# Chunk 0 of a retention block followed by an MLP: part 3 of w_in loaded ahead of the rows of batch 3, and M1 of chunk 0 reordered around it

## The chip, the cores and the metric

The kernel runs on one core of one Trainium2 chip. A core has five engines, each with its own in-order instruction stream: TensorE (matrix products, PE in the profile; PEld is its loading of weights), VectorE (DVE), ScalarE (ACT), GpSimd (POOL) and SyncE (SP, which here only issues DMAs). Engines wait for each other by semaphores. TensorE writes its results to PSUM[...]; VectorE or ScalarE must read ("evict") a bank before it can be used again. The metric is the device time of one execution, in microseconds, lower is better.

## The reference

Two layers, one after the other, in float32:

```python
# q, k, v: (4 batches, 8 heads, 768 steps, 64)
for t in range(768):
    state = gamma[h] * state + outer(k[t], v[t])        # 64 x 64 per batch and head
    y[t] = scale * q[t] @ state
x = y as (4 * 768 tokens, 512)
h = x @ w_in                                            # 512 x 2048
g = 0.5 * h * (1 + tanh(c * (h + 0.044715 h^3)))        # gelu
out = g @ w_out                                         # 2048 x 512
```

gamma is 1 - 2^(-5-head), and scale is 1/8.

## The kernel before, in words

**Tiling.** The 768 steps are cut into 6 chunks of 128. A chunk holds 4 batches of 128 tokens, so 512 tokens. All of a chunk's attention, then M1 (x times w_in, with gelu), then M2 (times w_out) is done before its result is stored; the attention of the next chunks is laid between the products of the chunk at hand. Operands are float16, accumulation is float32.

**Attention of one chunk and batch.** `prep1` casts the rows to float16 with the decay factors (L159, or L143 where a plain copy is enough). `mm_T` transposes q and k on TensorE (L188), 4 head pairs each, into one PSUM bank, and `ev_T` evicts it to `qkT`. `mm_A` multiplies k and q to scores (L208); `ev_A` evicts them with the causal mask (L221). `mm_yi` multiplies the scores with v (L243), `mm_yc` adds what comes from the earlier state (L230; nothing in chunk 0), and `ev_Y` evicts the result to `xT`, the transposed input of M1. `mm_s` multiplies k with v (L267) and `ev_S` folds it into the state. Each `ev_` function takes the engine that does it: VE is VectorE, AC is ScalarE.

**M1.** d_ff = 2048 is 16 blocks of 128 rows (fc). A block of h needs 4 matmuls (kc), one per 128 rows of w_in (L351). Two helpers cut the tokens of chunk 0: `moe1_two` does two blocks for 256 tokens (8 matmuls of 256 columns), `moe1_four` does four blocks for the 128 tokens of one batch (16 matmuls of 128 columns). Both fill one bank of the two with tag "h", and one gelu on ScalarE (L371) empties it into `g`. The token ranges are `t01` (batches 0 and 1), `t2`, `t3` and, before the change, `t23` (batches 2 and 3).

**M2.** The product g times w_out is done with seven products of half-size blocks in place of eight. `g_sums` and `w_sums` make the sums of blocks of g and of w_out that it needs (L401, results `s_g` and `t_w`). For chunk 0 the products are in `units_0`, a list of 15 units; most products are at L632, those at L665 follow after a bank has been kept. Unit 6 ends the first product and keeps it as `s_p` (a ScalarE copy, L643); unit 7, the first at L665, goes on in the same bank. The call of `run(units_0(), ...)` gives for each unit what is done after it: after unit 3 `preps(1, 0)`, the casts of q and k of chunk 1, batch 0, on ScalarE; after unit 5 `att_T(0)`, the transposes of chunk 1, batch 0, with their eviction.

**The order** is written out by hand, line by line, and each engine does its own instructions in that order. Loads of rows come from SP and ACT at first. The weights are cast from float32 to float16 on their way, by DMAs that GpSimd issues: w_in in four parts of 4 blocks each (part 1 in two halves; the code counts from 0, so `load_w_in(2)` is the third part), then w_out in four parts. Rows of batch 3 and of chunk 1 are issued by GpSimd as well, in one stream with the weights. GpSimd also casts k of batch 3 (`prep1(PO, "k", 0, 3)`), and stands at that cast until the row has come; the loads of w_out are behind it. The `spin` calls are products of zeros, whose result nobody reads.

Of the kernel before, what the change touches and what calls it, by code (L numbers as in the profile page):

```python
# [16 lines left out]
def kernel(  # L17
# [11 lines left out]
    C = 128  # L29
# [4 lines left out]
    NF = d_ff // 128  # L34
# [44 lines left out]
    def ld_tile(nm, c, b):  # L79
        if (nm, c, b) not in raw:  # L80
            tag, n = ("v1" if nm == "v" else "qk1", 5 if nm == "v" else 8) if c == 1 else (f"{nm}32", 4)
            raw[nm, c, b] = ld.tile([128, H, Dh], F32, tag=tag, bufs=n, name=f"{nm}32")
        return raw[nm, c, b]
# [30 lines left out]
    def spin(n):  # L114
        ps = bank("h", shape=(128, 512), name="spin_ps")
        for _ in range(n):
            nc.tensor.matmul(
                out=ps, lhsT=zero[:, 0:128], rhs=zero, start=True, stop=True
            )
# [21 lines left out]
    def copy_on(eng, out, in_):  # L141
        if eng is nc.scalar:
            eng.copy(out=out, in_=in_)  # L143
        else:
            eng.tensor_copy(out=out, in_=in_)

    def prep1(eng, nm, c, b):
        if nm == "v":
            t = pre.tile([128, H, Dh], F16, tag="v16", bufs=6, name="v16")
        else:  # L150
            if (c, b) not in qk16:
                qk16[c, b] = pre.tile([128, 2, H, Dh], F16, tag="qk16", bufs=6, name="qk16")
            t = qk16[c, b][:, "qk".index(nm)]
        src = ld_tile(nm, c, b)
        if (nm == "v") == (c < 1):
            copy_on(eng, t, src)
        else:
            col = OQ if nm == "q" else OK
            eng.tensor_tensor(  # L159
                out=t,  # L160
                in0=src,
                in1=cst[:, col:col + H].unsqueeze(2).broadcast_to([128, H, Dh]),
                op=ALU.mult,
            )
        h16[nm, c, b] = t
# [11 lines left out]
    def bank(tag, dt=F32, shape=(128, NHP, 128), name="ps"):  # L177
        return psum.tile(list(shape), dt, tag=tag, bufs=BANKS[tag], name=name)
# [24 lines left out]
    def mm_A(c, b):  # L203
        t = qkT[c, b]
        ps = [bank("att", name=f"a_ps{j}") for j in range(2)]
        for hp in range(NHP):
            for j in range(2):
                nc.tensor.matmul(  # L208
                    out=ps[j][:, hp],
                    lhsT=t[j * 64:(j + 1) * 64, 1, hp],  # L210
                    rhs=t[j * 64:(j + 1) * 64, 0, hp],
                    start=True,
                    stop=True,
                )
        pss["A", c, b] = ps

    def ev_A(c, b):
        ps = pss.pop(("A", c, b))
        for j in range(2):
            s = att.tile([128, NHP, 128], F16, tag=f"a{j}", bufs=2, name=f"a_sb{j}")  # L220
            nc.vector.tensor_tensor(out=s, in0=ps[j], in1=mask[:, j], op=ALU.mult)  # L221
            a_sb[c, b, j] = s

    def mm_yc(c, b, tag):
        y_ps = pss["Y", c, b] = bank(tag, name="y_ps")
        if c == 0:
            return

        for hp in range(NHP):
            nc.tensor.matmul(  # L230
                out=y_ps[:, hp],
                lhsT=st[:, b, hp].rearrange("p j d -> p (j d)"),
                rhs=qkT[c, b][:, 0, hp],
                start=(hp == 0),
                stop=False,
                skip_group_check=True,
            )
# [14 lines left out]
    def ev_Y(c, b, eng=nc.vector):  # L252
        if c not in xT:
            xT[c] = xp.tile([128, NHP, B * C], F16, tag="x", bufs=2, name="xT")
        x, ps = xT[c][:, :, b * C:(b + 1) * C], pss.pop(("Y", c, b))
        if c < 1:
            copy_on(eng, x, ps)
        else:
            nc.vector.tensor_tensor(out=x, in0=ps, in1=dec, op=ALU.mult)  # L259
# [15 lines left out]
    def ev_S(c, bs, engs=(nc.vector, nc.vector)):  # L275
        if c + 1 >= NCk:
            return
        s_ps = pss.pop(("S", c, bs))
        for j in range(2):
            sl = slice(j * 64, (j + 1) * 64)  # L280
            t = st[sl, bs[0]:bs[-1] + 1, :, j]
            if c == 0:
                copy_on(engs[j], t, s_ps[sl])
                continue
            for hp in range(NHP):
                nc.vector.scalar_tensor_tensor(  # L286
                    out=t[:, :, hp],
                    in0=t[:, :, hp],
                    scalar=cst[sl, OG + hp:OG + hp + 1],
                    in1=s_ps[sl, :, hp],  # L290
                    op0=ALU.mult,
                    op1=ALU.add,
                )
# [35 lines left out]
    def load_w_in(i, r0=0, r1=4):  # L329
        n0 = w_in_at[i] + r0  # L330
        nc.gpsimd.dma_start(  # L331
            out=w_in_sb[i][:, :, r0 * 128:r1 * 128],
            in_=moe_w_in.rearrange("(kc p) n -> p kc n", p=128)[
                :, :, n0 * 128:(n0 + r1 - r0) * 128
            ],
        )
# [41 lines left out]
    def moe1_two(c, fp, t0, t1):  # L378

        h_ps = bank("h", shape=(128, 2, B * C // 2), name="h_ps")  # L380
        for r in range(2):
            moe1_mm(c, 2 * fp + r, h_ps[:, r, 0:t1 - t0], t0, t1)
        gelu(g_tile(c, 2 * fp)[:, :, t0:t1], h_ps[:, :, 0:t1 - t0])

    def moe1_four(c, fq, t0, t1):
        h_ps = bank("h", shape=(128, 4, C), name="h_ps")
        for r in range(4):
            moe1_mm(c, 4 * fq + r, h_ps[:, r], t0, t1)
        r0 = fq % 2 * 4
        gelu(g_sb[fq // 2][:, r0:r0 + 4, t0:t1], h_ps)  # L390
# [12 lines left out]
    def w_sums(i):  # L403
        t = {j: t_w[j][:, 2 * i:2 * i + 2] for j in t_w}
        tt(nc.vector, t[1], w_q(i, 0, 1), w_q(i, 0, 0), ALU.subtract)
        tt(nc.vector, t[3], w_q(i, 1, 1), w_q(i, 0, 1), ALU.subtract)
        tt(nc.vector, t[2], w_q(i, 1, 1), t[1], ALU.subtract)
        tt(nc.vector, t[4], w_q(i, 1, 0), t[2], ALU.subtract)

    def g_sums(eng, c, f0, f1, p0=0, p1=2, keys=(1, 2, 3, 4)):  # L410
        i = f0 % 4
        q = {
            (r, b): g_q(c, r, b, f0 // 4)[:, i:i + f1 - f0, p0:p1]
            for r in range(2)
            for b in range(2)
        }
        t = {j: s_g[j][:, f0:f1, p0:p1] for j in s_g}
        ops = (
            (1, q[0, 1], q[1, 1], ALU.add),
            (2, t[1], q[0, 0], ALU.subtract),  # L420
            (3, q[0, 0], q[0, 1], ALU.subtract),
            (4, q[1, 0], t[2], ALU.subtract),
        )
        for j, in0, in1, o in ops:
            if j in keys:
                tt(eng, t[j], in0, in1, o)
# [284 lines left out]
    def loads(eng, c, *what):  # L711
        for nm, b in what:
            load1(eng, nm, c, int(b))
# [7 lines left out]
    VE, AC, PO, SY = nc.vector, nc.scalar, nc.gpsimd, nc.sync  # L721
    half = 2 * C
# [9 lines left out]
    prep1(PO, "k", 0, 1)  # L732
    load_w_in(0, 2, 4)
    load_w_in(1)
    loads(PO, 0, "k3", "q3", "v3")
    load_w_in(2)
    load_w_in(3)
    prep1(PO, "k", 0, 3)
    for i in range(NO):
# [9 lines left out]
    ev_T(0, 1, AC)  # L749
    prep1(AC, "v", 0, 0)  # L750
    spin(4)
    mm_A(0, 1)
    ev_A(0, 1)
    mm_yc(0, 0, "o")
    mm_yi(0, 0)
    prep1(AC, "v", 0, 1)
    ev_Y(0, 0, AC)
    prep1(VE, "q", 0, 2)
    prep1(VE, "k", 0, 2)
    spin(3)  # L760
    mm_yc(0, 1, "o")
    mm_yi(0, 1)
    mm_s(0, (0, 1), "o")
    ev_Y(0, 1, AC)
    spin(2)

    t01, t2, t3, t23 = (0, half), (half, half + C), (half + C, 2 * half), (half, 2 * half)
    moe1_two(0, 0, *t01)
    mm_T(0, 2)
    ev_T(0, 2)  # L770
    prep1(AC, "v", 0, 2)
    moe1_two(0, 1, *t01)
    mm_A(0, 2)
    ev_A(0, 2)
    ev_S(0, (0, 1), (AC, VE))
    moe1_two(0, 2, *t01)
    mm_yc(0, 2, "o")
    mm_yi(0, 2)
    ev_Y(0, 2)
    moe1_two(0, 3, *t01)  # L780
    prep1(VE, "q", 0, 3)
    moe1_four(0, 0, *t2)
    mm_T(0, 3)
    ev_T(0, 3)
    prep1(AC, "v", 0, 3)
    moe1_four(0, 1, *t2)
    mm_A(0, 3)
    ev_A(0, 3)
    g_sums(VE, 0, 0, 4, 0, 1)
    moe1_two(0, 4, *t01)  # L790
    moe1_two(0, 5, *t01)
    mm_yc(0, 3, "o")
    mm_yi(0, 3)
    mm_s(0, (2, 3))
    ev_Y(0, 3)
    ev_S(0, (2, 3))
    moe1_two(0, 6, *t01)
    moe1_two(0, 7, *t01)

    nc.gpsimd.tensor_copy(out=dec[0:1, 0, 0:1], in_=w_out_sb[3][0:1, 0, 0:1])  # L800
    nc.sync.dma_start(out=dec.rearrange("p h t -> p (h t)"), in_=dec_h.ap())
# [4 lines left out]
    g_sums(VE, 0, 4, 8, 0, 1)  # L806
    for fq in range(2):
        moe1_four(0, fq, *t3)
    w_sums(1)
    g_sums(VE, 0, 0, 4, 1, 2)  # L810
    for fp in range(4, NF // 2):
        moe1_two(0, fp, *t23)

    def prep_kT(c, b):
        prep1(AC, "k", c, b)
# [30 lines left out]
    def rows_of(c):  # L846
        for b in range(B):
# [6 lines left out]
            0: [(g_sums, VE, 0, 4, 8, 1, 2), (w_sums, 2)],  # L854
            1: [(w_sums, 3)],
            3: [(preps, 1, 0)],
            5: [(att_T, 0)],
            6: [(preps, 1, 1)],
            7: [(att_1A, 0)],
            8: [(att_T, 1), (preps, 1, 2)],  # L860
# [214 lines left out]
```

## Time and profile before

The time is 202.81 us, the median of 3 runs (202.48 to 202.95). The profiled execution has a span of 200.5 us.

| Engine | Busy, us | Share of the span |
|---|---|---|
| TensorE (PE) | 192.2 | 96% |
| weight load (PEld) | 153.2 | 76% |
| VectorE | 135.0 | 67% |
| ScalarE | 117.1 | 58% |
| GpSimd | 136.5 | 68% |

| Stretch, us | TensorE busy | VectorE | ScalarE | GpSimd |
|---|---|---|---|---|
| 0 to 13 | 10.47 | 6.62 | 5.71 | 9.93 |
| 13 to 26 | 11.08 | 8.64 | 6.25 | 8.35 |
| 26 to 33 | 7.00 | 6.05 | 4.68 | 2.15 |
| 33 to 40 | 6.76 | 6.39 | 2.71 | 5.22 |
| 40 to 60 | 20.00 | 16.78 | 12.09 | 10.62 |

How to read it: the first table is an average over the whole; the second shows where TensorE is not full. A stretch in which an engine is busy for its whole length sets the pace there; in the others it waits for something, and the chain of waits and the timeline tell for what. Busy times of TensorE include the overlap of its pipeline, so a full stretch is not the peak of the unit.

In lines of the profile, `out<-in` are the names of tiles in the code, "x16" is a number of instructions, and the bracket at the end is the idle time just before and what ended it.

### The profile page before, as it was taken

Reading aid. Unit: us, or ns where it says so; the run is one execution under the profiler, and the core shown is the slowest. Engines: PE = TensorE matmul, PEld = TensorE weight load, DVE = VectorE, ACT = ScalarE, POOL = GpSimd, SP = SyncE. Lnnn points to the kernel's source line nnn. Section 1 sums busy time; section 2 is a strip of 40 time slices with the busy share of each in tenths; the row PEclk is TensorE's granted clock in tenths of the full one; section 3 lists DMA queues with packets and bytes.
Section 4 is the critical chain, followed back from the end, with each engine's and each line's share of the span. In section 5 each row is a group of like instructions: output and inputs, shape, how many; then the busy total and the mean of one; then the engine's idle time right before and its main releaser. Section 6 shows DMA issues by size and latency. Waiting matters only on the chain.

```text
span 200.5 us, 5124 instructions
## 1 busy us (share of the span) xinstructions
PE 192.2 (96%) x2070; PEld 153.2 (76%) x2070; DVE 135.0 (67%) x281; ACT 117.1 (58%) x213; POOL 136.5 (68%) x139
## 2 busy tenths in 40 slices
PE   7797899999999999999999999999999999999993
PEld 2365798887887888745577888888888888888882
DVE  3566789869792459995996965995835935227720
ACT  2464554563689419255748698289484495867211
POOL 6782943845199999669969429299979299598100
PEclk9999999999999999999999999999999999999999
DMA  7999999999998899999999589830400220002204
GB/s 159 284 216 272 206 206 253 344 336 207 307 227 163 202 219 224 198 274 261 217 212 239 121 200 216 143 147 32 105 3 0 105 108 0 3 0 106 108 26 183
DMA packets 84743, 34.25 MB, mean 171 GB/s; under 512 B 76976, under 2 KB 81968, under 8 KB 84720
## 3 DMA queue, kind: packets, MB, share of 16 engines
q1 hardware_dynamic: 72736, 18.91, 43.1%
q0 software_dynamic: 7392, 13.37, 25.6%
q10 hardware_dynamic: 4592, 1.65, 3.2%
q8 instruction: 16, 0.26, 0.5%
q14 instruction: 7, 0.06, 0.1%
HBM read 27.63 MB, written 6.29 MB: 169 GB/s over the span
## 4 chain that ended last, share of the span: by engine, by line
PE 84%; DMA 8%; POOL 3%; DVE 2%; ACT 1%; issue 1%; SPq 1%; DVEq 0%
PE o_ps L512 31%; PE h_ps L594 19%; PE h_ps L351 18%; DMA w_in<-in_moe_w_in_dram 5%; PE o_ps L632 3%; PE y_ps L243 3%; PE a_ps L208 3%; PE o_ps L665 3%; DMA k<-in_k_dram 3%; PE y_ps L230 2%; PE s_ps L267 1%; DVE a_sb L221 1%; PE qkT_ps L188 1%; POOL w_in L331 1%; POOL qk L159 1%; DVE xT L259 1%
## 5 line engine op out<-in xcount | busy, mean ns | idle before, releaser
L351 PE MATMUL h_ps<-xT,w_in 128*128 128x256 f16 (+2 forms) x352 | 45.9, 282 | 1.7 <-DMA w_in<-in_moe_w_in_dram 1.5
L371 ACT ACTIVATE g<-h_ps 128x512 f16<-128x512 f32 x52 | 30.9, 599 | 22.5 <-PE h_ps L351 20.8
L221 DVE TENSOR_TENSOR a_sb<-a_ps,mask 128x512 f16<-128x512 f32 x48 | 30.5, 682 | 15.4 <-PE a_ps L208 12.8
L401 POOL TENSOR_TENSOR s_g<-g 128x512 f16<-128x512 f16 x30 | 35.2, 1180 | 7.5 <-ACT g L371 6.5
L351 PEld LDWEIGHTS <-w_in 128*128 128x128 f16 x352 | 30.4, 98 | 12.8 <-DMA w_in<-in_moe_w_in_dram 2.4
L512 PEld LDWEIGHTS <-s_g 128*128 128x128 f16 x320 | 30.6, 98 | 4.2 <-POOL s_g L401 0.3
L371 ACT ACTIVATE g<-h_sb 128x512 f16<-128x512 f32 x36 | 21.9, 632 | 17.4 <-DVE h_sb L401 17.3
L512 PE MATMUL o_ps<-t_w,s_g 128*128 128x256 f16 x240 | 29.4, 273 | 0.0
L401 DVE TENSOR_TENSOR h_sb<-h_ps,h_sb 128x512 f32<-128x512 f32 x36 | 22.8, 682 | 9.6 <-ACT h_sb L143 8.9
L159 POOL TENSOR_TENSOR v<-v,cst 128x512 f16<-128x512 f32 x20 | 20.5, 1046 | 4.3 <-PE y_ps L230 2.5
L512 PEld LDWEIGHTS <-g 128*128 128x128 f16 x208 | 20.2, 98 | 2.5
L401 POOL TENSOR_TENSOR s_g<-s_g,g 128x512 f16<-128x512 f16 x18 | 20.9, 1162 | 1.4
L401 POOL TENSOR_TENSOR s_g<-g,s_g 128x512 f16<-128x512 f16 x18 | 20.6, 1156 | 0.0
L594 PEld LDWEIGHTS <-t_in 128*128 128x128 f16 x192 | 18.0, 98 | 2.9
L143 ACT COPY h_sb<-h_ps 128x512 f32<-128x512 f32 x36 | 19.1, 598 | 1.3 <-PE h_ps L594 1.3
L512 PE MATMUL o_ps<-w_out,g 128*128 128x256 f16 x160 | 19.1, 273 | 0.0
L286 DVE SCALAR_TENSOR_TENSOR st<-st,cst,s_ps 64x128 f16<-64x128 f16 x64 | 18.2, 346 | 0.2
L594 PE MATMUL h_ps<-s_x,t_in 128*128 128x256 f16 x144 | 17.8, 273 | 0.0
L259 DVE TENSOR_TENSOR xT<-y_ps,dec 128x512 f16<-128x512 f32 x20 | 13.3, 682 | 5.4 <-PE y_ps L243 5.4
L594 PEld LDWEIGHTS <-w_in 128*128 128x128 f16 x144 | 14.1, 98 | 1.8
L143 ACT CAST qk<-q 128x512 f16<-128x512 f32 x20 | 12.6, 630 | 3.0 <-DMA q<-in_q_dram 3.0
L401 POOL TENSOR_TENSOR s_g<-g,g_odd 128x512 f16<-128x512 f16 x6 | 6.9, 1153 | 9.0 <-ACT h_sb L143 9.0
(83 smaller groups left out, 274.3 us busy)
## 6 DMA issues: line engine op xcount, KB each, us to landing
out_dram<-o_sb POOLq DMA_DIRECT2D x10, 512.0 KB, 3.1
k<-in_k_dram SPq DMA_DIRECT2D x19, 256.0 KB, 4.7
v<-in_v_dram SPq DMA_DIRECT2D x18, 256.0 KB, 4.2
q<-in_q_dram SPq DMA_DIRECT2D x16, 256.0 KB, 4.7
w_out<-in_moe_w_out_dram POOLq DMA_DIRECT2D x4, 512.0 KB, 10.6
w_in<-in_moe_w_in_dram POOLq DMA_DIRECT2D x3, 512.0 KB, 10.0
k<-in_k_dram POOLq DMA_DIRECT2D x5, 256.0 KB, 8.8
q<-in_q_dram POOLq DMA_DIRECT2D x5, 256.0 KB, 8.6
```

The costliest lines, as they stand in the source:

```text
L143: eng.copy(out=out, in_=in_)
L159: eng.tensor_tensor(out=t, in0=src, in1=cst[:, col:col + H].unsqueeze(2).broadcast_to([128, H, Dh]), op=ALU.mult,)
L208: nc.tensor.matmul(out=ps[j][:, hp], lhsT=t[j * 64:(j + 1) * 64, 1, hp], rhs=t[j * 64:(j + 1) * 64, 0, hp], start=True, stop=True,)
L221: nc.vector.tensor_tensor(out=s, in0=ps[j], in1=mask[:, j], op=ALU.mult)
L243: nc.tensor.matmul(out=y_ps[j * 64:(j + 1) * 64, hp], lhsT=h16["v", c, b][:, 2 * hp + j], rhs=a_sb[c, b, j][:, hp], start=(c == 0), stop=True,
L259: nc.vector.tensor_tensor(out=x, in0=ps, in1=dec, op=ALU.mult)
L286: nc.vector.scalar_tensor_tensor(out=t[:, :, hp], in0=t[:, :, hp], scalar=cst[sl, OG + hp:OG + hp + 1], in1=s_ps[sl, :, hp], op0=ALU.mult, ...
L351: nc.tensor.matmul(out=out, lhsT=w_in_sb[wi][:, kc, wr * 128:(wr + 1) * 128], rhs=xT[c][:, kc, t0:t1], start=(kc == 0), stop=(kc == NHP - ...
L371: nc.scalar.activation(out=out, in_=in_, func=AF.Gelu_apprx_tanh, scale=1.0)
L401: eng.tensor_tensor(out=out, in0=in0, in1=in1, op=op)
L512: nc.tensor.matmul(out=po, lhsT=lhs(c, lk, fp, a), rhs=rhs(rk, fp), start=(new and fp == 0 and (last or a == 0)), stop=(stop and fp == NP ...
L594: nc.tensor.matmul(out=self.ps[G, k][:, p], lhsT=self.lhs(lk, 2 * G + p, kc), rhs=self.rhs(rk, kc), start=(new and p == 0 and kc == 0), st ...
```

## The change

The third part of w_in is issued ahead of the rows of batch 3 instead of behind them. M1 of chunk 0 is put in another order: batches 0 to 2 are multiplied with the first three parts of w_in before the pieces of batch 3, and batch 3 (t3) is done for all 16 blocks at the end, in four units of four blocks; the units for t23 are gone. The casts of q and k of batch 2 on VectorE, and the cast of its v on ScalarE, are put earlier; two spins are dropped. Three kinds of eviction go from VectorE to ScalarE: y of batch 3, both halves of the state of batches 2 and 3, and the transposes of batch 0 of chunk 1. The purpose is to give TensorE work on the weights that have come while it waits for the rest.

```diff
@@ loads
     load_w_in(0, 2, 4)
     load_w_in(1)
+    load_w_in(2)
     loads(PO, 0, "k3", "q3", "v3")
-    load_w_in(2)
     load_w_in(3)
     prep1(PO, "k", 0, 3)
@@ attention of batches 0 and 1, then M1
     spin(4)
+    prep1(VE, "q", 0, 2)
     mm_A(0, 1)
     ev_A(0, 1)
+    prep1(VE, "k", 0, 2)
     mm_yc(0, 0, "o")
     mm_yi(0, 0)
     prep1(AC, "v", 0, 1)
     ev_Y(0, 0, AC)
-    prep1(VE, "q", 0, 2)
-    prep1(VE, "k", 0, 2)
     spin(3)
...
     ev_Y(0, 1, AC)
-    spin(2)
-
-    t01, t2, t3, t23 = (0, half), (half, half + C), (half + C, 2 * half), (half, 2 * half)
-    moe1_two(0, 0, *t01)
+    prep1(AC, "v", 0, 2)
+
+    t01, t2, t3 = (0, half), (half, half + C), (half + C, 2 * half)
     mm_T(0, 2)
     ev_T(0, 2)
-    prep1(AC, "v", 0, 2)
-    moe1_two(0, 1, *t01)
+    moe1_two(0, 0, *t01)
     mm_A(0, 2)
     ev_A(0, 2)
-    ev_S(0, (0, 1), (AC, VE))
-    moe1_two(0, 2, *t01)
+    moe1_two(0, 1, *t01)
     mm_yc(0, 2, "o")
     mm_yi(0, 2)
     ev_Y(0, 2)
+    ev_S(0, (0, 1), (AC, VE))
+    moe1_two(0, 2, *t01)
+    moe1_four(0, 0, *t2)
     moe1_two(0, 3, *t01)
+    g_sums(VE, 0, 0, 4, 0, 1)
+    moe1_four(0, 1, *t2)
     prep1(VE, "q", 0, 3)
-    moe1_four(0, 0, *t2)
+    moe1_two(0, 4, *t01)
+    moe1_two(0, 5, *t01)
     mm_T(0, 3)
     ev_T(0, 3)
     prep1(AC, "v", 0, 3)
-    moe1_four(0, 1, *t2)
+    moe1_four(0, 2, *t2)
     mm_A(0, 3)
     ev_A(0, 3)
-    g_sums(VE, 0, 0, 4, 0, 1)
-    moe1_two(0, 4, *t01)
-    moe1_two(0, 5, *t01)
+    moe1_two(0, 6, *t01)
+    moe1_two(0, 7, *t01)
     mm_yc(0, 3, "o")
     mm_yi(0, 3)
     mm_s(0, (2, 3))
-    ev_Y(0, 3)
-    ev_S(0, (2, 3))
-    moe1_two(0, 6, *t01)
-    moe1_two(0, 7, *t01)
+    ev_Y(0, 3, AC)
+    ev_S(0, (2, 3), (AC, AC))
+    moe1_four(0, 3, *t2)
@@ end of M1
     for fq in range(2):
         moe1_four(0, fq, *t3)
+    g_sums(VE, 0, 0, 4, 1, 2)
     w_sums(1)
-    g_sums(VE, 0, 0, 4, 1, 2)
-    for fp in range(4, NF // 2):
-        moe1_two(0, fp, *t23)
+    for fq in range(2, 4):
+        moe1_four(0, fq, *t3)
@@ M2 of chunk 0, what follows unit 5
-            5: [(att_T, 0)],
+            5: [(att_T, 0, AC)],
```

## The prediction

> **What bounds the kernel now.** I read the page first: TensorE is busy for 192.2 of 200.5 us, and the stage table gives it 20.00 of the 20 us from 40 to 60, 39.85 of 40 from 60 to 100, and all of 100 to 190. Only the opening has holes: 10.47 of 13 us, then 11.08 of 13, and 6.76 of the 7 us from 33 to 40. So whatever moves the opening's end moves the whole. Next the chain that ended last, for the opening; columns are start, length, and what the time went to:
>
> ```profile
> 12.60 10.02 DMA w_in<-in_moe_w_in_dram
> 22.62 0.05 issue
> 22.67 1.94 PE h_ps L351 x16
> ...
> 25.27 7.20 PE h_ps L351 x80
> 32.47 5.24 PE o_ps L632 x48
> 37.71 0.45 PE qkT_ps L188 x8
> 38.15 0.45 PE o_ps L632 x4
> 38.60 0.02 issue
> 38.62 0.59 ACT s_p L643
> 39.22 0.04 issue
> 39.26 1.03 PE o_ps L665 x8
> ```
>
> The third part of w_in lands at 22.62. From 25.27 TensorE is solid to 38.6, waits for one copy (s_p) on ScalarE, and goes on at 39.26. What frees it at 25.27 is in the timeline (start, length, engine, instructions, idle before):
>
> ```profile
> 22.67 1.64 PEld L351 LDWEIGHTS <-w_in 128*128 128x128 f16 x16 [0.56 <-DMA w_in<-in_moe_w_in_dram]
> ...
> 25.26 6.92 PEld L351 LDWEIGHTS <-w_in 128*128 128x128 f16 x80 [0.19 <-DMA w_in<-in_moe_w_in_dram]
> ...
> 26.35 0.60 ACT L371 ACTIVATE g<-h_ps 128x512 f16<-128x512 f32 x1 [1.12 <-PE h_ps L351]
> 27.22 0.60 ACT L371 ACTIVATE g<-h_ps 128x512 f16<-128x512 f32 x1 [0.28 <-PE h_ps L351]
> 28.11 0.60 ACT L371 ACTIVATE g<-h_ps 128x512 f16<-128x512 f32 x1 [0.30 <-PE h_ps L351]
> 29.01 0.60 ACT L371 ACTIVATE g<-h_ps 128x512 f16<-128x512 f32 x1 [0.30 <-PE h_ps L351]
> 29.88 0.60 ACT L371 ACTIVATE g<-h_ps 128x512 f16<-128x512 f32 x1 [0.28 <-PE h_ps L351]
> ```
>
> The fourth part of w_in lands at about 25.25; its DMA was issued at 13.35 and took 11.9. So the gate is the arrival of the last part, not the order of TensorE before it. The gelu starts are a ruler: a unit of 8 matmuls of 256 columns takes 27.22-26.35 = 0.87 us, one of 16 matmuls of 128 columns 29.01-28.11 = 0.90. A gelu begins 1.08 us after its unit (26.35-25.27).
>
> The last view is a comparison of one kind of eviction on two engines:
>
> ```profile
> 6.30 1.01 ACT L143 COPY qkT<-qkT_ps 128x1024 f16<-128x1024 f16 x1 [1.01 <-PE qkT_ps L188]
> ...
> 38.19 0.69 DVE L145 COPY qkT<-qkT_ps 128x1024 f16<-128x1024 f16 x1
> 38.62 0.58 ACT L643 COPY s_p<-o_ps 128x512 f32<-128x512 f32 x1 [1.12 <-PE o_ps L632]
> ```
>
> The transposed q and k of chunk 1 are evicted by VectorE while ScalarE, idle for 1.12 us, waits to take s_p.
>
> [...] The trace agrees with an ordered stream: w_in parts at 16.95, 22.62 and 25.25, batch 3's rows between the first two at 18.8, 19.4 and 20.1.
>
> **The change part by part.**
>
> *The DMA order.* Part 3 of w_in (512 KB) now goes ahead of three row loads (256 KB each). Queue time, from landings: a w_in part 2.5 to 2.6 us (25.25-22.62), the three rows 3.15 (20.1-16.95). So part 3 lands at 16.95+2.6 = 19.5, k of batch 3 at 21.3, q at 22.0, v at 22.7, and part 4 again at 25.25: the same bytes stand before it. The queue stays fed, because part 4 is still issued at about 13.3. Behind it, GpSimd casts k of batch 3 (1.04 us) before it issues w_out; that cast moves from 18.79 to about 21.3, w_out's first issue from 19.78 to 22.4. Part 4 occupies the queue to about 25, so I take no gap; the other bound is in the rivals.
>
> *Before the gate.* TensorE has after 12.4 us: six wide units (6 x 0.87), three narrow ones (3 x 0.90), two sets of transposes (0.45 each, from the chain) and two of scores (0.33), one of y (0.34), in all 9.8 us against 12.9 to the gate. The dropped two spins (0.6 us busy) and the earlier units fall in this slack. The q cast of batch 2 moves ahead of an eviction on VectorE, but q landed at 3.88+5.9 = 9.8 and the cast (0.69) ends at 10.5, when the eviction could start at 10.46: nothing. Batch 3's last pieces: q cast by 22.7, transposes to 23.15, unit of part 3 to 24.05, scores to 24.4. All done 0.85 before the gate. These edits cost and bring nothing: waiting for part 4 hides them.
>
> *After the gate, TensorE.* Before: eight units, 6 wide and 2 narrow: 6 x 0.87 + 2 x 0.90 = 7.02. After: two wide and five narrow units, plus y and the state product of batch 3, which used to lie ahead of the gate (0.34 and 0.37): 1.74+4.5+0.71 = 6.95. So 0.07 less (0.1 with unrounded gelu starts).
>
> *After the gate, ScalarE.* Here three evictions are added: y of batch 3 and both halves of the state product. In ScalarE's order they stand between the second wide unit's gelu and the next one. Starts on ScalarE follow each other 0.49 to 0.52 us apart (gelu 13.93, cast 14.43; gelu 15.55, cast 16.05). The second gelu starts at 27.22, y at 27.72, the state halves at 28.21 and 28.70, and only then the first narrow unit's gelu, at 29.2 to 29.8. That unit is multiplied by 28.6, and the next, in the other of two banks, by 29.5. The third narrow unit needs the first's bank and waits to 29.84: 0.3 us. Its successors lose nothing more. Sum at the end of M1: +0.3-0.1 = +0.2 us. If ScalarE took the full durations one after the other (0.60, 0.58, 0.57, 0.57) the wait would be 0.75; if the states came late behind the gelu, none. I take +0.2, and keep -0.1 and +0.65.
>
> VectorE loses these evictions (3 x 0.69), but its s_g sums for batches 2 and 3 now stand ahead of w_sums(1) and wait for the gelu of the second t3 unit, which ends at 31.5. From there it has g_sums (1.4 us), w_sums(1) (1.5), g_sums (1.4), w_sums(2) and (3) (1.5 each): the operand t_w[2] of the first L665 product is complete at about 38.5, and that product starts at 39.9. The first product with a t_w operand (L632, at 34.3) needs the first operation of w_sums(1), done at 33.4. Nothing, by 0.9 us or more.
>
> *The eviction of chunk 1's first transposes moves to ScalarE.* This one is on the path. Transposes begin at 37.54 in the timeline (the chain's 37.71 deducts overlap); an eviction starts 0.65 later (38.19); on ScalarE the following copy can start 0.91 after it (6.30 apart: in the opening 8.96 to 9.87). So s_p starts at T+1.56 and, at 0.58+0.06, TensorE goes on at T+2.20. Before: 39.26-37.54 = T+1.72. Cost +0.48. Queued behind it on ScalarE are the casts of the next batch (39.11), wanted only at 41.4, and what waits for it is the product at L665, the whole of TensorE.
>
> An earlier T couldn't help much either: the last cast of chunk 1's k starts at 36.89, 0.14 idle after its predecessor, as its row landed at 36.87, and ends at 37.51, when the transposes begin. The rows bound that point to within 0.05 us.
>
> Sum: +0.2+0.5 = +0.7 us; 202.81+0.7 = 203.5. After 39.26 TensorE has no idle time that would take it up.
>
> **The rivals.** (1) *The queue runs dry.* If k of batch 3 lands only with v (22.7), GpSimd issues w_out at 23.8[...]. Chunk 1's rows come that much later, the transposes wait some 0.6: 204.1. For it: GpSimd waits for k now for 4.63 us with w_out behind it. Against it: w_out's first part landed 2.5 after part 4, back to back, with 3 us of lead. (2) *The evictions on ScalarE fit.* No bank wait; M1 ends 0.1 earlier; the handover of s_p costs 0.48: +0.4, 203.2, at the edge of no change. (3) *The gate moves.* Part 4 and the rows behind it arrive earlier, because the rows next to part 3 move better in the new place, and TensorE's fuller slack then counts. To beat both costs the stream must gain over 0.8 us; 1.3 us gained gives 202.3, faster. For it: k of batch 3 took 1.8 us after part 2, q and v 0.65 each, so the change of kind costs something. Against it: there are as many such changes in the new order.
>
> **How the numbers follow.** Forecast +0.7 (203.3 to 203.8): 0.6. Rival 1: 0.13. Rival 2: 0.13. Rival 3: 0.14. The range leaves out most of rival 3 and the far end of rival 1: 202.7 to 204.3; the full ScalarE times (+0.65+0.48 = 203.9) lie in it. Bound of no change is 0.4 us: faster takes rival 3 (0.14), the same takes most of rival 2 (0.12), slower the rest (0.74).
>
> **What would show it.** In the changed kernel: part 4 released at 25.2 to 25.3; three ScalarE copies between two gelus near 28; a TensorE wait for ScalarE inside the narrow units of 0.3 us; the 1.01 us copy of qkT on ScalarE just ahead of s_p; the first L665 product at about 39.95. A last part that lands at 24.5, or that product at 39.3 or sooner, makes me wrong.

## The result and the profile after

The changed kernel takes 205.1 us (median of 4 runs, 204.67 to 205.37) against 202.84: slower by 2.3 us, ratio 1.0113 with a 95% interval of 1.0090 to 1.0135. The profiled executions differ by 3.0 us in span (203.5 and 200.5). In part of the runs of some experiments TensorE's granted clock is lowered (in the profiled ones it falls to half for 3.4 or 6.8 us in the opening), and most of these take 1 to 6 us longer; medians below are of all runs, ratios leave out runs over 1.5% above the kernel's fastest.

First the chain that ended last, of the changed kernel (start, length, what the time went to):

```profile
10.50 10.36 DMA k<-in_k_dram
20.86 0.07 issue
20.93 1.04 POOL qk L159
21.97 2.97 POOL w_out L340 x4
24.95 0.85 POOL q L86
25.80 13.78 DMA k<-in_k_dram
39.58 0.02 issue
39.60 0.63 ACT qk L143
40.23 0.05 issue
40.28 0.41 PE qkT_ps L188 x4
40.69 0.02 issue
40.71 1.01 ACT qkT L143
41.72 0.50 ACT s_p L643
42.22 0.04 issue
42.26 1.03 PE o_ps L665 x8
```

Before, a part of w_in (the third, as the chain has it) and then TensorE itself made this chain. Now it runs from batch 3's k, over GpSimd's cast and the issue of w_out behind it, to the row of chunk 1's k, which lands at 39.58 instead of 36.87. M1 and M2's first units are no longer on it.

The rate at which the DMA engines moved data is the last column of the table by stretches (busy times of the engines, then TensorE's clock, DMA share, GB/s). The kernel before:

```profile
22.00:24.00 2.00, 1.61 (x21) 1.30 (x18) 1.65 (x4) 0.83 (x2) 2.00 (x4) 1.00 1.24 206
24.00:26.00 2.00, 1.92 (x37) 1.51 (x35) 2.00 (x5) 0.95 (x2) 1.99 (x3) 1.00 1.24 206
26.00:28.00 2.00, 2.00 (x29) 1.89 (x28) 1.19 (x3) 1.19 (x2) 0.39 (x1) 1.00 1.26 212
```

The changed kernel:

```profile
22.00:24.00 2.00, 1.18 (x11) 0.81 (x9) 1.95 (x5) 1.45 (x4) 2.00 (x3) 1.00 1.04 170
24.00:26.00 2.00, 1.96 (x34) 1.74 (x35) 0.77 (x2) 0.72 (x2) 2.00 (x4) 1.00 0.98 142
26.00:28.00 2.00, 2.00 (x30) 1.64 (x30) 1.21 (x2) 1.01 (x3) 2.00 (x3) 1.00 1.13 157
28.00:30.00 2.00, 2.00 (x51) 1.96 (x46) 0.96 (x3) 1.96 (x5) 1.19 (x2) 1.00 1.13 183
```

From 22 to 32 the stream carries 376 KB less than before (five stretches of 2 us: 170, 142, 157, 183, 192 against 206, 206, 212, 202, 206), which at 206 GB/s is 1.8 us of the 2.7 by which chunk 1's k is late: about 1.0 from 22 to 26, where the queue runs dry, and 0.85 in the slow stream after it. That is the hole that the prediction said would not be there. Another 0.65 us comes last: k lands 1.41 us after q of the same batch (39.58 and 38.17), before the change 0.76. The hole isn't the reason for this; in e3, below, which has the same loads, it is 0.77, and in e10, which has no hole, 1.59.

TensorE's own path is late too. The timeline of the kernel before:

```profile
16.98 0.77 PEld L351 LDWEIGHTS <-w_in 128*128 128x128 f16 x8 [1.31 <-DMA w_in<-in_moe_w_in_dram]
37.10 0.60 PE L632 MATMUL o_ps<-w_out,s_g 128*128 128x256 f16 x4
37.54 0.61 PE L188 MATMUL qkT_ps<-iden,qk 128*128 128x128 f16 x8
```

The changed kernel:

```profile
17.72 5.18 PEld L351 LDWEIGHTS <-w_in 128*128 128x128 f16 x64 [1.62 <-DMA w_in<-in_moe_w_in_dram]
21.20 1.05 DVE L401 TENSOR_TENSOR s_g<-g 128x512 f16<-128x512 f16 x1 [3.49 <-ACT g L371]
23.30 0.68 DVE L159 TENSOR_TENSOR qk<-q,cst 128x512 f16<-128x512 f32 x1
24.04 0.45 PEld L188 LDWEIGHTS <-qk 128*128 128x128 f16 x8 [1.14 <-DVE qk L159]
25.82 1.64 PEld L351 LDWEIGHTS <-w_in 128*128 128x128 f16 x16
30.59 2.84 PE L351 MATMUL h_ps<-xT,w_in 128*128 128x128 f16 x48 [0.36 <-ACT g L371]
33.26 1.91 PE L632 MATMUL o_ps<-w_out,g 128*128 128x256 f16 x16
38.07 0.60 PE L632 MATMUL o_ps<-w_out,s_g 128*128 128x256 f16 x4
38.87 0.23 PEld L188 LDWEIGHTS <-qk 128*128 128x128 f16 x4 [0.48 <-ACT qk L143]
```

Part 2 of w_in releases TensorE at 17.72 (16.98 before). The cast of batch 3's q stands on VectorE behind four sums, which wait for a gelu until 21.20, though q landed at 21.6; so the transposes start at 24.04, and the first unit of part 4 at 25.82, with no wait for a DMA: the part landed at 24.85 (13.15+11.7). M2 begins at 33.26 instead of 32.30.

The 3.0 us at the first L665 product (42.26 against 39.26) split as follows. TensorE reaches the transposes of chunk 1 at 38.51 (38.07 and a unit of 0.44) instead of 37.54: +0.97. The transposes of k start at 40.28 instead of 0.22 after that, because the row is late: +1.55, of which 0.65 is the gap between q and k. The product follows them by 1.98 instead of 1.50, because of the eviction on ScalarE: +0.48.

### The profile page after: what moved, and what is told of

Same layout as the page of the kernel before. It is cut to its first block, busy times and chain, and to the rows that moved or that the text cites. A ratio compares the mean times of both kernels' runs of the same rounds, so it can differ in the third digit from the quotient of the medians.

```text
span 203.5 us, 5181 instructions
## 1 busy us (share of the span) xinstructions
PE 192.5 (95%) x2100; PEld 153.7 (76%) x2100; DVE 132.6 (65%) x277; ACT 119.6 (59%) x217; POOL 136.3 (67%) x139
## 3 DMA queue, kind: packets, MB, share of 16 engines
q10 hardware_dynamic: 4592, 1.65, 3.1%
## 4 chain that ended last, share of the span: by engine, by line
PE 76%; DMA 14%; POOL 4%; DVE 2%; ACT 1%; issue 1%; SPq 1%; DVEq 0%
PE o_ps L512 31%; PE h_ps L594 19%; DMA k<-in_k_dram 14%; PE h_ps L351 13%; PE y_ps L243 3%; PE a_ps L208 3%; PE o_ps L665 3%; PE y_ps L230 2%; POOL w_out L340 1%; POOL qk L159 1%; PE s_ps L267 1%; POOL w_in L331 1%; DVE a_sb L221 1%; PE qkT_ps L188 1%; DVE xT L259 1%
## 5 line engine op out<-in xcount | busy, mean ns | idle before, releaser
L351 PEld LDWEIGHTS <-w_in 128*128 128x128 f16 x384 | 31.0, 98 | 12.5 <-DMA w_in<-in_moe_w_in_dram 2.1
L594 PEld LDWEIGHTS <-w_in 128*128 128x128 f16 x144 | 14.1, 98 | 1.8
L143 ACT CAST qk<-k 128x512 f16<-128x512 f32 x20 | 12.6, 630 | 0.8 <-DMA k<-in_k_dram 0.8
```

The source lines that it names most:

```text
L351: nc.tensor.matmul(out=out, lhsT=w_in_sb[wi][:, kc, wr * 128:(wr + 1) * 128], rhs=xT[c][:, kc, t0:t1], start=(kc == 0), stop=(kc == NHP - ...
L594: nc.tensor.matmul(out=self.ps[G, k][:, p], lhsT=self.lhs(lk, 2 * G + p, kc), rhs=self.rhs(rk, kc), start=(new and p == 0 and kc == 0), st ...
```

## The experiments

Theory Q at first: the queue ran dry, because GpSimd's cast, and the issue of w_out behind it, moved with the row; the eviction on ScalarE comes on top. Its rivals: the order of the transfers itself (O), the new order of M1 (M), a hidden eviction (N).

**e2, the load order alone, in the kernel before.**

```diff
+    load_w_in(2)
     loads(PO, 0, "k3", "q3", "v3")
-    load_w_in(2)
```

> The kernel before, with only the load order changed: part 3 of w_in ahead of the rows of batch 3; no change of M1 or of any eviction. Theory Q: GpSimd's cast of k moves to 21, w_out is issued near 22, k of chunk 1 lands near 39.5 and the time rises by 1.5 to 2.2 us to 204.4 to 205.0, less than the whole change by the 0.5 us of the ScalarE eviction. Theory M (the order of M1 and the evictions on ScalarE cost the time): 202.6 to 203.1.

204.45 us, ratio 1.0099 (1.0076 to 1.0122). w_out is issued at 22.38, the rate in the two microseconds from 23 is 131 and 74 GB/s, and chunk 1's k is cast at 39.11. Two swapped lines make most of the loss; M1's new order and the evictions aren't needed for it. But the time met theory Q's forecast in part by luck, for TensorE comes just as late by itself:

```profile
39.10 0.60 PE L632 MATMUL o_ps<-w_out,s_g 128*128 128x256 f16 x4
39.54 0.64 PE L188 MATMUL qkT_ps<-iden,qk 128*128 128x128 f16 x8
```

The transposes follow TensorE's own unit at once (39.10 and 0.44), and the cast of k ends at 39.73, just when its transposes are due. In the old order of M1, batch 3's transposes stand ahead of units of parts 2 and 3, and now wait until 23.04 for their row; the first unit of part 4 starts at 27.26 and M2 at 34.30, both 2.0 us late.

**e5, the issue of w_out made late, with the old order of transfers.**

```diff
     prep1(PO, "k", 0, 3)
+    nc.gpsimd.memset(late, 0.0)
+    nc.gpsimd.memset(late, 0.0)
     for i in range(NO):
         load_w_out(i)
```

> The kernel before, with two extra memsets of 1024 columns on GpSimd, some 1.8 us, between its cast of k of batch 3 and its loads of w_out; load order, M1 and evictions as before. Theory Q: the late issue alone empties the queue; w_out is issued near 21.6, the rate falls below 180 GB/s for some us after 23, k of chunk 1 lands 1.2 to 2.5 us later and the time rises by 1.0 to 2.2 us, to 203.8 to 205. Theory O: a late issue with the old order of transfers is hidden by the queue's lead of 3 us, and the time stays within 0.4 us of 202.8.

204.14 us, ratio 1.0077 (1.0060 to 1.0094). w_out is issued at 22.82. By stretches:

```profile
24.00:26.00 2.00, 2.00 (x32) 1.64 (x32) 1.97 (x6) 0.85 (x2) 2.00 (x4) 1.00 0.73 117
26.00:28.00 2.00, 1.91 (x33) 1.65 (x29) 1.99 (x4) 0.87 (x2) 2.00 (x3) 1.00 1.18 189
28.00:30.00 2.00, 2.00 (x36) 1.98 (x35) 1.04 (x4) 1.27 (x3) 2.00 (x3) 1.00 1.15 191
```

The same hole without any change in what is moved: late issue alone makes it. In steps of 1 us the rate is 155, 54 and 179 from 23, so most of the old work ends between 23 and 24 and new bytes come some 2 us after the issue. As in the changed kernel, the stream then stays below 206 for about 8 us; what keeps it there no run shows. What the hole costs in time e5 doesn't show: in its profiled run the opening is 1.1 us late before the edited lines count (from 4 to 8 us TensorE does 14 products in 3.17 us busy, in the kernel before 27 in 3.45; part 4 lands at 26.34 instead of 25.22, and M2 begins at 33.43 instead of 32.30). That is most of the 1.64 us at the first L665 product; the rows add the other 0.5 (transposes of k at 39.39, where TensorE was ready at 38.89).

**e1, the changed kernel with w_out issued ahead of the cast.**

```diff
-    prep1(PO, "k", 0, 3)
     for i in range(NO):
         load_w_out(i)
+    prep1(PO, "k", 0, 3)
```

> The changed kernel, with the four loads of w_out issued ahead of GpSimd's cast of k of batch 3 instead of behind it. Theory Q (the DMA queue ran dry, because w_out was issued only after that cast): w_out is issued by about 17, the queue moves about 206 GB/s without a gap from 22 to 33, k of chunk 1 lands at 36.5 to 37.3 instead of 39.6, the transposes of chunk 1 start when M2's units let them, near 38.5, and the time falls by 1.2 to 1.6 us to about 203.6. Theory O (the order of the transfers itself is slower, or they disturb each other): k of chunk 1 still lands near 39.5 and the time stays within 0.4 us of 205.1.

The hole is gone (208, 208, 207, 205 and 207 GB/s from 22 to 32) and k of chunk 1 is cast at 37.17, 2.4 us sooner: with the new order of transfers the queue stays full when the issue is early, so theory O falls for the hole. The time is 204.53 us, ratio 1.0101 (1.0074 to 1.0127): hardly better. In the profiled execution, the slowest of its runs (205.79), TensorE's clock was 0.57 from 18 to 22; the runs at a clock of 0.998 or more took 203.67 to 204.88. So Q alone is not enough. Theory S took its place: TensorE's own path and the rows run late side by side, and mending one leaves the other.

**e11, e2 with the same edit as e1**, to test S where M1 is old.

> The kernel before with part 3 of w_in ahead of batch 3's rows, as in the run of the load order alone, and w_out issued ahead of the cast of k, so that the queue does not run dry. Theory S (two delays side by side: TensorE's own path is as late as the rows): k of chunk 1 lands 2 us sooner, yet the transposes start within 0.5 us of where they did, and the time stays at 204.0 to 204.5. Theory Q alone: 202.6 to 203.1.

```profile
37.20 0.62 ACT L143 CAST qk<-k 128x512 f16<-128x512 f32 x1
40.03 0.61 PE L188 MATMUL qkT_ps<-iden,qk 128*128 128x128 f16 x8
```

The row is there 1.9 us sooner than in e2, and the transposes start 0.5 us later than in e2 (39.54). The time is 205.7, ratio 1.0106 (1.0075 to 1.0137); the seven fastest of 18 runs lie at 204.03 to 204.46, the others, many of them with a lowered clock, at 205.2 to 207.4. Part 2 lands at 18.55 here, batch 3's transposes wait 1.72 us for the cast of q, and the first unit of part 4 starts at 27.75. The time that S gave, 204.0 to 204.5, is met by those seven alone, but the start of the transposes is as it said: S holds; Q alone, at 202.6 to 203.1, doesn't.

**e3 and e7, the eviction by itself**: given back to VectorE in the changed kernel (e3), given to ScalarE in the kernel before (e7).

```diff
-            5: [(att_T, 0)],
+            5: [(att_T, 0, AC)],
```

> The changed kernel, with the eviction of chunk 1's first transposes given back to VectorE. Theory H (the handover of s_p costs 0.48 us, wherever the transposes start): the first L665 product starts 0.4 to 0.5 us sooner after the transposes of k, and the time falls by that, to about 204.6. Theory N (the wait for chunk 1's rows hides the eviction): no change, 204.9 to 205.3.

> The kernel before, with the eviction of chunk 1's first transposes on ScalarE and nothing else changed. Theory H (that eviction stands ahead of s_p and costs 0.48): the first L665 product starts 2.0 us after the transposes of k instead of 1.5, the time rises by 0.4 to 0.5, to 203.0 to 203.1. Theory N (hidden): 202.4 to 202.7.

e3: 204.31 us, ratio 1.0085 (1.0066 to 1.0104) where the change has 1.0113. e7: 202.95 us, ratio 1.0019 (0.9999 to 1.0039). The times alone don't quite settle 0.5 us; the timeline of e7 does:

```profile
38.27 0.61 PE L188 MATMUL qkT_ps<-iden,qk 128*128 128x128 f16 x8
38.92 1.01 ACT L143 COPY qkT<-qkT_ps 128x1024 f16<-128x1024 f16 x1 [0.65 <-PE qkT_ps L188]
39.83 0.59 ACT L643 COPY s_p<-o_ps 128x512 f32<-128x512 f32 x1
40.47 1.03 PE L665 MATMUL o_ps<-t_w,s_g 128*128 128x256 f16 x8 [0.71 <-ACT s_p L643]
```

The product comes 2.20 us after the transposes, 1.72 in the kernel before: 0.48. (The transposes themselves start 0.73 later in this run, at 38.27, as part 4 lands at 25.95.) In e3 it comes 1.51 us after those of k (39.71 and 41.22), in the changed kernel 1.98. The wait for the rows hides nothing of it, since the eviction comes after that wait.

**e4, e1 and e3 together.**

> The changed kernel with w_out issued ahead of the cast of k, and the eviction of chunk 1's first transposes back on VectorE. Theory S (three costs: the rows of chunk 1 and TensorE's own path run late side by side, the eviction comes on top of the later of them): k of chunk 1 lands by 37.3, the transposes start when M2's units let them, near 38.8, the first L665 product follows 1.7 us later, and the time is 203.7 to 204.1, some 0.5 below the run with w_out ahead alone. What is left over 202.6 is TensorE's path in M1. Theory Q alone (the empty queue and the eviction are all there is): 202.6 to 203.0.

The ratio is 1.0089 (1.0056 to 1.0122). The three runs at a clock of 0.998 or more took 203.52, 203.61 and 203.89 us, and a fourth at 0.996 took 204.75; the five at 0.989 to 0.992 took 205.93 to 207.25, and the median, 205.93, is one of these. In the profiled run TensorE waits to 18.13 for part 2 and then runs at half its clock. At full clock the forecast is met, within a tenth or two, and 1 us over the kernel before is left.

**e6, the changed kernel with the old load order.**

> The changed kernel with the old load order: rows of batch 3 ahead of part 3 of w_in; M1 and the evictions as changed. Theory P (a part of w_in lands late when another part stands right behind it): part 2 lands 7.7 us after its issue as in the kernel before, where the changed kernel has 8.6; w_out is issued near 19.8, the queue has no gap, k of chunk 1 lands near 36.9. M1's new order costs by itself, because part 3 comes at 22.6 with the pieces of batch 3 behind its units: the first unit of part 4 starts near 26.1 instead of 25.3 and the first L665 product near 40.7; time 203.7 to 204.3. Rival (the load order was all of it, but for the eviction): that unit starts at 25.3, time 202.9 to 203.2.

204.05 us, ratio 1.0093 (1.0061 to 1.0125). No hole, k of chunk 1 cast at 36.73, and yet the loss: part 3 comes at 22.51, its two units are followed by batch 3's transposes (24.27), and the first unit of part 4 starts at 26.03, the product at L665 at 40.91. So M1's new order costs by itself under the old loads, as forecast. Of the 1.65 us at that product, 1.17 is M1 (transposes at 38.71 instead of 37.54) and 0.48 the eviction. So the load order alone costs 1.9 us (e2), M1's order with the evictions 1.5 (e6), and both together 2.3: the two overlap. Part 2 took 8.9 us from its issue, not 7.7: theory P fell.

**e9, e4 with the q cast first and four spins in the wait for part 2.**

```diff
+    spin(4)
     moe1_two(0, 2, *t01)
...
+    prep1(VE, "q", 0, 3)
     g_sums(VE, 0, 0, 4, 0, 1)
     moe1_four(0, 1, *t2)
-    prep1(VE, "q", 0, 3)
```

> The changed kernel with w_out ahead, the transposes' eviction on VectorE, the cast of q of batch 3 ahead of the sums on VectorE, and four spins in TensorE's wait for part 2[...]. Theory V (the cast of q, queued behind sums that wait for a gelu, holds up batch 3's transposes by 0.9 us, and these the units of part 4): the transposes follow the units of part 3 within 0.2 us, the first unit of part 4 starts when that part lands, the granted clock stays at 0.997 or more, and the time is 202.7 to 203.1. Rival (the cast's place costs nothing): 203.5 to 203.9, as in the undisturbed runs of the version without these two edits.

203.31 us beside 203.17 for the kernel before in this series, ratio 1.0004 (0.9982 to 1.0026). By that ratio nearly all of the loss is gone, but the kernel before was slower in this series (71 runs) than in the series of e1 on the same chip (202.58, 11 runs), and in e9's trace the first L665 product comes at 40.18, still 0.92 later than in the kernel before (39.26). All 22 runs have a clock of 0.997 or more. The transposes follow at 23.32, without a wait; but the scores then wait 0.63 us, as the eviction of the transposes has taken the cast's place behind the sums, and the first unit of part 4 starts at 25.78, as in the changed kernel (25.82), not when the part lands (25.28). The forecast of the wait was right, those of the gate and of the time (202.7 to 203.1) weren't. The two edits were made together, so no run tells what either is worth.

**e10, e9 with y and the states of batch 3 evicted by VectorE.**

```diff
-    ev_Y(0, 3, AC)
-    ev_S(0, (2, 3), (AC, AC))
+    ev_Y(0, 3)
+    ev_S(0, (2, 3))
```

> The same, with y of batch 3 and both halves of the state evicted by VectorE again, as in the kernel before. Theory A (the three ScalarE evictions delay a gelu and TensorE waits 0.36 us for its bank): that wait goes, and the time is 0.3 lower than in the run beside it, 202.4 to 202.8. Rival (VectorE, now fuller, delays a sum or the y): no lower.

```profile
32.52 1.91 PE L632 MATMUL o_ps<-w_out,g 128*128 128x256 f16 x16
37.73 0.60 PE L632 MATMUL o_ps<-t_w,s_g 128*128 128x256 f16 x4 [0.59 <-DVE t_w L401]
40.32 1.03 PE L665 MATMUL o_ps<-t_w,s_g 128*128 128x256 f16 x8 [0.24 <-ACT s_p L643]
```

The ScalarE wait is gone and M2 begins at 32.52 (33.22 in e9), but VectorE's sums of w_out come later, TensorE waits 0.59 for them, and the product at L665 starts no sooner (40.32, 40.18 in e9). The median, 206.05, ratio 1.0072 (1.0035 to 1.0109), is not explained by this: the runs spread from 203.03 to 208.45, and the profiled one took 203.44. Nine of the 22 have a clock of 0.992 or less, although the four spins are there as in e9, and took 206.83 or more; the other 13 still spread from 203.03 to 206.58. The rival is right on where the gain went; the spread stays open.

**e8 and e12, a version from these findings.** k and q of batch 3 stand ahead of part 3, v behind it, so that no part waits long and w_out is issued at 19.69; the first unit of batch 2 fills the wait for part 2; the sums stand behind the scores of batch 3; evictions are as before the change. e8 has in addition the first rows of chunk 1 ahead of the last part of w_out; e12 hasn't.

```diff
-    load_w_in(2)
-    loads(PO, 0, "k3", "q3", "v3")
+    loads(PO, 0, "k3", "q3")
+    load_w_in(2)
+    loads(PO, 0, "v3")
...
+    moe1_four(0, 0, *t2)
     moe1_two(0, 2, *t01)
-    moe1_four(0, 0, *t2)
     moe1_two(0, 3, *t01)
-    g_sums(VE, 0, 0, 4, 0, 1)
-    moe1_four(0, 1, *t2)
     prep1(VE, "q", 0, 3)
+    moe1_four(0, 1, *t2)
+    mm_T(0, 3)
+    ev_T(0, 3)
     moe1_two(0, 4, *t01)
+    prep1(AC, "v", 0, 3)
+    mm_A(0, 3)
+    ev_A(0, 3)
+    g_sums(VE, 0, 0, 4, 0, 1)
     moe1_two(0, 5, *t01)
...
-    for i in range(NO):
+    for i in range(NO - 1):
         load_w_out(i)
-    loads(PO, 1, "q0", "k0", "q1", "k1", "v0", "v1", "q2", "k2")
+    loads(PO, 1, "q0", "k0")
+    load_w_out(NO - 1)
+    loads(PO, 1, "q1", "k1", "v0", "v1", "q2", "k2")
...
```

> A new version: k and q of batch 3 between parts 2 and 3 of w_in, v between parts 3 and 4; q and k of chunk 1, batch 0, ahead of the last part of w_out; M1 with batch 2's first unit ahead of part 2, the transposes of batch 3 after part 2's units, its scores and y spread between the units of part 3, so that only parts 4's units for batches 0 to 2 and the four of batch 3 are left when part 4 lands; all evictions as before the change. Theory S and P together: part 2 lands 7.7 us after its issue, part 3 near 21.6, part 4 near 25.3; M2 starts at 31.5 instead of 32.3, k of chunk 1 lands near 34.5 and holds nobody up, the first L665 product starts near 38.5; time 201.5 to 202.2, faster than the kernel before by about 0.8. Rival (the last part of w_out, now later, or VectorE's sums hold M2 up): 202.4 or more.

> The new version with q and k of chunk 1, batch 0, behind the last part of w_out again, as in the kernel before. Theory R (those rows, which land at 36.9, bound the transposes once M1 ends sooner): the transposes of k start near 37.7 and the time is 0.4 to 0.6 higher than that of the new version, 202.3 to 202.5, no faster than 0.2 us under the kernel before. Rival: 201.8 to 202.0.

e8: 201.89 us beside 202.55, ratio 0.9965 (0.9954 to 0.9977), all 9 runs within 0.5 us: faster than both kernels. Its timeline:

```profile
25.66 6.39 PE L351 MATMUL h_ps<-xT,w_in 128*128 128x256 f16 x96
31.88 1.91 PE L632 MATMUL o_ps<-w_out,g 128*128 128x256 f16 x16
37.12 0.61 PE L188 MATMUL qkT_ps<-iden,qk 128*128 128x128 f16 x8
38.84 1.03 PE L665 MATMUL o_ps<-t_w,s_g 128*128 128x256 f16 x8 [0.24 <-ACT s_p L643]
```

M2 begins at 31.88, 0.4 sooner than in the kernel before, and the first L665 product as well; 0.7 was forecast for the product. Part 2 took 8.8 us from its issue, not the 7.7 of the forecast. e12: 202.45 beside 203.17, ratio 0.9951 (0.9930 to 0.9971). The two ran on different chips, and their intervals overlap, so the times don't separate them; its timeline does show what was forecast: transposes of k at 37.84 after a wait for their cast, and the product at 39.34, 0.5 later than in e8. That is no sooner than in the kernel before (39.26), and e12's ratio rests on the 203.17 of e9's series: that e12 is faster than the kernel before is not shown.

**e13 to e16, why part 2 lands late.** Its landing is 7.7 to 8.0 us after its issue in the kernel before, e5 and e7, and 8.6 to 9.4 in most others. Each run puts one thing of the change into the kernel before: the casts of q and k of batch 2 (e13), no `spin(2)` (e14), both with batch 2's transposes and scores ahead (e15), v of batch 3 behind part 3 (e16).

> The kernel before, with the casts of q and k of batch 2 on VectorE put as in the change. Theory C (they slow the queue's last pieces): part 2 lands 8.6 or more after its issue. Theory L (only what stands behind part 2 in the queue counts) and theory N (a spread from run to run): 7.7 to 8.0, and the time within 0.3 us of the kernel before.

> The kernel before without its two spins ahead of M1. They lie in a wait, so the time stays within 0.3 us of the kernel before, and part 2 lands 7.7 to 8.0 after its issue by theories L and C. A landing at 8.6 or more would speak for N, since nothing that moves data is changed.

> The kernel before with the casts, the transposes and the scores of batch 2 as early as in the change, and no spins before M1; loads as before. Theory M (what the engines do up to 17 us delays part 2): it lands 8.6 or more after its issue, as with the new M1 and the old loads. Theory L: 7.7 to 8.0. The gate of part 4 stays, so the time is within 0.4 us of the kernel before.

> The kernel before with k and q of batch 3 ahead of part 3 of w_in and v behind it. Theory L: part 2, with rows right behind it, lands 7.7 to 8.0 after its issue; theory N: anything from 7.7 to 9.4. w_out is issued near 19.8, and the queue does not run dry; the time is within 0.4 us of the kernel before.

Landings: 7.7 in e13, 9.2 in e14, 8.7 in e15, 8.0 in e16. e13 gives no sign that the casts matter; e14, where nothing that moves data differs, and e6 (8.9 with rows behind) speak against the order as the only cause. Over all profiles it is 7.7 to 9.2 with rows right behind part 2 (ten kernels, median 8.4) and 8.1 to 9.4 with part 3 behind it (eight, median 8.9). The two overlap and each kernel has one profile: whether the order adds to the spread is left open. The medians are 202.92, 202.46, 203.74 and 202.95 us beside 202.49, ratios 1.0021 (1.0005 to 1.0038), 1.0003 (0.9970 to 1.0036), 1.0041 (1.0018 to 1.0064) and 1.0015 (0.9992 to 1.0037); ten of e15's 18 runs have a clock of 0.992 or less. Of the forecasts for the time, only e14's holds (within 0.3 us of the kernel before); e13 is 0.43 above it (0.3 forecast), e15 1.25 and e16 0.46 (0.4 forecast), e16 with an interval that takes in no change.

## Why the prediction was wrong, step by step

- **Direction** right: slower was given 0.74. **Size** wrong: +0.7 forecast, +2.3 measured, outside the range that ended at 204.3.
- **"The queue stays fed ... so I take no gap"** is the first of two steps that failed. The cast did move to 20.93 and the issue to 21.92, even 0.4 sooner than forecast (21.3 and 22.4). But I held the issue against the landing of part 4. Most of its bytes were through by 23.6, where the rate falls (210 GB/s up to 23.2, 97 from 23.6 to 23.8), over a microsecond ahead of its landing at 24.85, and in e5 new bytes come some 2 us after the issue (issue at 22.82; 54 GB/s from 24 to 25, 179 from 25). By my estimate from these two, the issue had to come by about 21.6, and it came at 21.92. That is 0.3 us late, and the dip costs 1.0, because the rate takes from 23.2 to 23.8 to fall and is back at 206 only near 25.2. The rival with 0.13 was the case in its mechanism, though k of batch 3 did not land with v as it supposed (20.86 and 22.41), and the gap that it priced was an assumption of mine that the trace of before did not show. It was still too small at 204.1, since it had neither the slow stream after the hole nor the next point.
- **"All done 0.85 before the gate ... These edits cost and bring nothing"** is the other, and weighs about as much: with the queue full and the eviction back on VectorE, 1 us of the loss stays (e4). I took part 2 at 16.95 from one profile (17.72 in the changed kernel), and put the cast of q at the landing of q, without walking VectorE's queue: four sums ahead of it wait for a gelu. Slack of 0.85 became a delay of 0.55 over the kernel before. The cast's wait is shown (e9), but moving the cast alone did not bring the gate back: the sums then held the next piece, the eviction of the transposes. That VectorE's order and the late part 2 make up the 0.55 is read from the timeline; no run separates them.
- **After the gate, ScalarE**: right. Forecast a wait of 0.3 for the bank of the first narrow unit; measured 0.36, and e10 removes it by moving the evictions. What e10 also shows, and I had at "nothing": VectorE's sums have no room for these evictions in that order.
- **After the gate, TensorE**: 0.1 less was forecast. From the first unit of part 4 to M2 it is 7.44 us against 7.03; without the wait, 7.08. No gain.
- **The eviction of chunk 1's transposes**: right, 0.48 in three places (the changed kernel, e3, e7).
- **"The rows bound that point to within 0.05 us"**: near, and underused. The transposes of q come first, so k's row was needed 0.22 us later, at 37.76, and had about 0.26 to spare. A point that two paths reach within a quarter of a microsecond is late as soon as either is. I priced one path and called the other fed.
- **Sum**: of the 3.0 us of the profiled pair, TensorE's path is 0.97 (0.2 forecast), the rows 1.55 on top (0; 0.65 of it the gap between q and k), the eviction 0.48 (0.48).

Left open: the low rate for some 8 us after the hole, the gap between chunk 1's q and k, the spread of part 2's landing, and e10's median.

## What to carry to other kernels

When a transfer is put later in a queue, look at what the issuing engine does with its data, and at everything it issues behind that: here one cast of 1.04 us, which waited for its row until 20.93, held four loads. Measure the lead of an issue against the end of the bytes of the transfer in front, not against its landing (about 23.6 and 24.85 here). Where two paths meet within a few tenths of a microsecond, price both, and walk the in-order queue of each engine on them before saying that an edit costs nothing.

## What the runs showed of the hardware

TensorE's granted clock fell to half at some of its waits for part 2 and not at others. In e14's profiled run TensorE has no product from 15.9 to 18.27, and near the end of that wait, at 17.7, its granted clock, the number just after POOL's busy time and count (0.93, 0.50, 0.50, 0.50), falls to half:

```profile
16.00:18.00 2.00, 0.00 (x0) 0.00 (x0) 1.96 (x3) 0.71 (x2) 0.00 (x0) 0.93 1.10 341
18.00:20.00 2.00, 1.73 (x8) 1.03 (x8) 0.00 (x0) 0.00 (x0) 1.09 (x2) 0.50 1.16 235
20.00:22.00 2.00, 2.00 (x16) 1.38 (x16) 1.24 (x2) 0.60 (x1) 2.00 (x3) 0.50 1.24 206
22.00:24.00 2.00, 2.00 (x19) 1.88 (x18) 0.05 (x1) 0.60 (x1) 2.00 (x4) 0.50 1.24 206
```

Eight matmuls of 256 columns take 1.89 us there (at 18.27), 1.05 at full clock (at 14.57 in the same run). In the profiled runs the clock fell at the wait for part 2 when TensorE stood for 1.59 us (e4), 1.68 (e1), 2.32 (e14) and 2.36 (e15). It did not fall at 1.46 in the changed kernel, nor at 2.03 in e6, 2.52 in e11 and 2.55 in e2: the length of the wait alone does not decide. By the clock of the stretches, the half clock after the wait lasts 3.4 us in e1 and e4 and 6.8 us in e14. What decides whether and for how long it falls, no run shows.

Whether four spins in the wait keep the clock up is not shown: all 22 runs of e9 have 0.997 or more, where 5 of 9 runs of e4 fell to 0.992 or below, but e10 has the same spins and 9 of its 22 runs fell. In e8, where a unit of products fills most of that wait, and in e12, with the same order of M1, all 31 runs have 0.996 or more. In e4, whose wait is 1.59 us in the profiled run, the five runs at 0.992 or less took 205.93 us or more, the three at 0.998 or more 203.89 or less: a wait of TensorE for a DMA can go with a loss above its own length, and in some executions only.
